# A steady step of a convolution and MLP kernel listed in another order, item by item

## Chip, core and metric

The kernel runs on one core of one Trainium2 chip. The metric is the time of one execution on the device in microseconds (us); lower is better. Each engine of the core works through its own list of instructions: TensorE (PE in the profile; PEld is its loading of weights), VectorE (DVE), ScalarE (ACT), GpSimd (POOL) and SyncE (SP, which only issues DMAs). They wait for one another through semaphores.

## What is computed

x is (8, 4096, 192), weight (8, 7), w_in (192, 2048), w_out (2048, 192), all float32.

```python
w = exp(weight - weight.max(-1));  w = w / (w.sum(-1) + 1e-9)      # 7 taps for each of 8 heads
x_pad = concatenate([zeros((B, 6, D)), x], axis=1)
out = einsum("hk,bskhg->bshg", w, x_unf)       # causal convolution, 24 channels to a head
x = out.reshape(32768, 192)
h = x @ w_in
g = h * (1.0 / (1.0 + exp(-1.702 * h)))
return g @ w_out                               # (32768, 192)
```

## The kernel before

The work goes in 32 steps ("big"), each of 512 tokens of two sequences, one sequence on either half of the partitions. Both matrix products are formed from fewer products of sums of blocks, so beside the products there are many sums and copies. The schedule is written out by hand: each engine gets its instructions in the order in which the program lists them.

One steady step has two parts. In the first, R below, the 20 products of `TERMS` are taken twice (two halves v of the hidden width) and each on two PSUM banks h = 0, 1: 80 matrix products of 64 x 128 by 64 x 512 (`product1`, line 598). The two banks of one product use the two row halves of the array. The results, named a0 to a8 while they lie in PSUM, are copied out by ScalarE (`copy2`, lines 633 and 635; k0 to k9 are rooms in SBUF), combined by VectorE (`sum2`, line 639) and put through the gelu by ScalarE (lines 615 and 620) into blocks of g. `ORDER` lists these items: `(0, "prod", 14, "a3")` is product 14 of half 0 into PSUM tile a3. An item there does both banks, h = 0 and then 1. Four PSUM tiles of two banks are handed out through the list `free`, in the order of first use.

In the second part, C below, the second product is taken: 78 "mains", each three matmuls of 128 x 32 by 256 on column strips 0 to 2 of the array, and 78 "sides", single matmuls on strip 3 (`one_matmul`, line 855). Mains and sides read g blocks and sums of them. These g sums, 128 x 1024 on VectorE (`add_up`, lines 355 and 357; `("sum", 6, 8, "-", 6)` in `PLAN`), stand partly in R (`EARLY_G`), and six more are accumulating DMAs ("acc", line 831) that GpSimd issues. `go(n)` takes n times one main and then one side, and where a side product ends, ScalarE's copy of it (line 880) stands right behind. "seed" is a copy by ScalarE between PSUM and rooms (line 884), "join" a sum of 96 x 256 on VectorE, "turn" a transpose of results by VectorE (line 771), "store" the DMA out.

Beside these, the convolutions of the next steps are made: x is transposed by VectorE (line 438), ScalarE multiplies it by each tap (line 483), GpSimd adds the taps of two channel groups (`next_add`, line 501) and issues accumulating DMAs for the third ("tree", line 506). Ten sums of the resulting blocks ("vsum", `next_sum`, lines 355 and 357, on GpSimd in steady steps) follow, and SyncE's DMAs "cross" copy blocks to the other half of the partitions. The queues `adds`, `tree`, `sums_left`, `pieces`, `todo` and `ready` hold these items in a fixed order, and "tap", "add", "vsum", "cross" and "done" in `ORDER` and `PLAN` take the next one of a queue.

The first steps (0 and 1) have a list of their own, `OPENING`, except that the second part of step 1 is made by `PLAN`.

## Time and profile before

| what | value |
|---|---|
| time, median of 3 runs | 2263.2 us (2262.88 to 2263.72) |
| time of the profiled execution | 2262.78 us |
| its span | 2261.1 us |
| DMA, mean over the span | 132 GB/s, 298.05 MB in all |
| ScalarE, GpSimd busy | 76%, 47% of the span |
| clock granted to TensorE | 1.0 |

A row of the profile gives the line of the kernel, the engine, the operation, "out<-in" by the program's names (a PSUM tile is a "slot"), and the shape; then a count. Groups give busy us and the mean ns of one. Rows of the timeline begin with start and length in us, and like instructions behind one another share a row. "<-" ahead of a name in brackets, or behind a wait, names what ended an engine's idle time.

### The profile page before, as it was taken

How to read it: one execution, taken by the hardware profiler on the slowest of the kernel's cores; microseconds unless marked ns; L12 is line 12 of the kernel's file. 1: busy time of each engine (PE TensorE's matmuls, PEld its weight loads, DVE VectorE, ACT ScalarE, POOL GpSimd, SP SyncE). 2: the span in 40 equal slices, each digit the busy share in tenths (PEclk: the TensorE clock that was granted, in tenths of full speed). 3: DMA queues.
4: the chain of work that ended last, by engine and by line, in shares of the span. 5: the costliest groups of instructions: out<-in, count | busy, mean ns of one | idle time of the engine just before them, and what ended most of it. 6: DMA issues, size and time to landing. Idle time of an engine off the chain costs nothing.

```text
span 2261.1 us, 62136 instructions
## 1 busy us (share of the span) xinstructions
PE 2248.2 (99%) x24966; PEld 1552.0 (69%) x24966; DVE 1985.3 (88%) x2970; ACT 1707.7 (76%) x3233; POOL 1063.9 (47%) x1098
## 2 busy tenths in 40 slices
...
GB/s 198 174 158 133 125 114 150 143 128 127 121 131 159 128 128 126 111 160 140 125 132 114 141 152 128 129 124 118 163 134 128 124 114 151 144 127 103 104 92 71
DMA packets 275679, 298.05 MB, mean 132 GB/s; under 512 B 119104, under 2 KB 203328, under 8 KB 275392
## 3 DMA queue, kind: packets, MB, share of 16 engines
...
q10 hardware_dynamic: 1648, 0.39, 0.1%
...
## 4 chain that ended last, share of the span: by engine, by line
PE 96%; DVE 2%; ACT 1%; issue 1%; DMA 1%; POOL 0%; DVEq 0%; ACTq 0%; POOLq 0%; SPq 0%
PE slot L598 49%; PE slot L855 45%; PE slot L1120 1%; DVE g L357 1%; DMA g<-osbs 0%; PE slot L1115 0%; DVE room L357 0%; ACT g L615 0%; PE slot L946 0%; DVE room L639 0%; ACT w_form L483 0%; DMA xin<-in_x_dram 0%; DVE slot L639 0%; DVE room L355 0%; DVE osbs L771 0%
## 5 line engine op out<-in xcount | busy, mean ns | idle before, releaser
L598 PE MATMUL slot<-conv_t,w_in_s 64*128 64x512 f32 x5152 | 1147.4, 594 | 3.3 <-ACT room L633 1.5
L598 PEld LDWEIGHTS slot<-conv_t,w_in_s 64*128 64x128 f32 x5152 | 663.3, 186 | 474.6 <-issue 312.1
L855 PE MATMUL slot<-g,w_form 128*32 128x256 f32 x9672 | 894.2, 379 | 0.7 <-DVE room L357 0.7
L855 PEld LDWEIGHTS slot<-g,w_form 128*32 128x32 f32 x9672 | 575.6, 110 | 128.9 <-DVE room L357 2.1
L501 POOL TENSOR_TENSOR conv_t<-conv_t,g 128x512 f32<-128x512 f32 x354 | 449.0, 1275 | 88.4 <-ACT g L483 65.4
L855 PE MATMUL slot<-g,w_out_s 128*32 128x256 f32 x5952 | 467.5, 379 | 1.3 <-DVE g L357 0.8
L357 DVE TENSOR_TENSOR g<-g 128x1024 f32<-128x1024 f32 x372 | 450.4, 1224 | 8.0 <-DMA g<-osbs 1.0
L880 ACT COPY room<-slot 32x256 f32<-32x256 f32 x651 | 237.2, 364 | 289.8 <-PE slot L855 281.5
L639 DVE TENSOR_TENSOR room<-slot,room 128x512 f32<-128x512 f32 x620 | 383.6, 679 | 67.8 <-PE slot L598 67.8
L633 ACT COPY room<-slot 128x512 f32<-128x512 f32 x620 | 337.7, 595 | 77.7 <-PE slot L598 61.7
L483 ACT ACTIVATE g<-xt,cw 128x512 f32<-128x512 f32 x534 | 353.9, 715 | 3.7
L620 ACT ACTIVATE g<-room 128x1024 f32<-128x1024 f32 x248 | 265.7, 1071 | 79.0 <-DVE room L639 49.3
L615 ACT ACTIVATE g<-slot 128x512 f32<-128x512 f32 x528 | 282.5, 610 | 51.9 <-PE slot L598 32.8
L831 POOL DMA_DIRECT2D g<-g x124 | 128.1, 1038 | 355.0 <-PE slot L855 330.8
L639 DVE TENSOR_TENSOR slot<-slot,room 128x512 f32<-128x512 f32 x372 | 239.7, 689 | 53.8 <-PE slot L598 52.2
L855 PEld LDWEIGHTS slot<-g,w_out_s 128*32 128x32 f32 x5952 | 239.7, 110 | 43.2 <-DVE room L639 23.3
L355 POOL TENSOR_TENSOR conv_t<-conv_t 128x256 f32<-128x256 f32 x210 | 179.3, 860 | 129.2 <-PE slot L598 119.6
L855 PE MATMUL slot<-osbs,w_form 128*32 128x256 f32 x2232 | 229.5, 379 | 0.0
L506 POOL DMA_DIRECT2D g<-g x120 | 105.9, 883 | 238.1 <-ACT g L483 99.4
L855 PEld LDWEIGHTS slot<-osbs,w_form 128*32 128x32 f32 x2232 | 132.5, 110 | 23.6
L639 DVE TENSOR_TENSOR slot<-room,slot 128x512 f32<-128x512 f32 x124 | 79.8, 687 | 41.8 <-PE slot L598 41.8
L855 PE MATMUL slot<-room,w_form 128*32 128x256 f32 x1488 | 112.9, 379 | 0.0
...
## 6 DMA issues: line engine op xcount, KB each, us to landing
...
conv_t<-conv_t SPq DMA_DIRECT2D x186, 192.0 KB, 5.4
...
conv_t<-conv_t SPq DMA_DIRECT2D x186, 128.0 KB, 2.9
out_dram<-osbs SPq DMA_DIRECT2D x186, 128.0 KB, 2.7
...
```

Of the source, the lines that this page charges most:

```text
L355: eng.tensor_add(v(dst), v(a), v(b))
L357: eng.tensor_sub(v(dst), v(a), v(b))
L483: act.mul(home, conv_src(big, c, k), cw[:, c, k : k + 1])
L501: nc.gpsimd.tensor_add(dst, dst, home)
L598: nc.tensor.matmul(slot[h], w_in_s[halves[h], a, v * P : (v + 1) * P], src, start=first, stop=True, skip_group_check=True,)
L615: act.activation(dst[:, :, h, :], src[h].rearrange("p (o t) -> p o t", o=2), AF.Gelu_apprx_sigmoid, scale=float(sign),)
L620: act.activation(dst.rearrange("p o h t -> p h o t"), src.rearrange("p h (o t) -> p h o t", o=2), AF.Gelu_apprx_sigmoid, scale=float(sign),)
L633: act.copy(bank(dst, h), bank(src, h))
L639: op(*(bank(t, h) for t in (dst, a, b)))
L831: nc.gpsimd.dma_start(out=spot(dst), in_=spot(a), accum_op=ALU.add)
L855: nc.tensor.matmul(dst, w, t, start=first, stop=last, skip_group_check=True)
L880: act.copy(to, d)
```

## The change

Steps 2 to 31 are no longer made by `ORDER`, `PLAN` and the queues, but by one list `STEP`, in which each item is one instruction (or the three matmuls of a main, or the two or more DMAs of a transfer). A flattened step of before and `STEP` hold the same 477 items. `OPENING` is written out in the same way, down to the end of step 1, in the order that it had.

In `STEP`, a product, copy, sum or gelu names its bank as its last entry (0 or 1; None for a gelu over both), and the banks of one product may stand apart. `("m", i)` is main i, `("s", i)` side i, `("t", i)` the copy of the i-th finished side; they no longer alternate. `("gsum", ...)` is a g sum. For items of the convolution the first number says how many steps ahead the item works: `("add", 1, 2, 5)` adds tap 5 of channel group 2 of the next step, `("vsum", 1, 9)` is its vsum 9. The three chunks of a side product lie in the strip-3 parts of three PSUM tiles; these are now taken in the order by, bx, bs in place of bx, bs, by.

The core of the diff:

```diff
-    ORDER = [
-        (0, "prod", 6, "a8"), (0, "sum", "k0", "a8", "-", "k8"), (0, "prod", 2, "a3"), (0, "copy", "k4", "a3", 1),
-        (0, "prod", 12, "a2"), ("tap",), ("tap",), ("tap",), ("tap",), ("add", 4), (0, "prod", 16, "a0"),
-        (0, "sum", "a1", "a2", "-", "k0"), ("add", 4), ("turn", 0), (0, "prod", 14, "a3"), (0, "copy", "k1", "a0", 1),
-        (0, "prod", 9, "a2"), (0, "sum", "a4", "a2", "-", "k1"), (0, "prod", 3, "a1"), (0, "copy", "k2", "a1", 1),
-        (0, "prod", 15, "a3"), (0, "prod", 7, "a4"), (0, "prod", 1, "a1"), (0, "sum", "k3", "a4", "+", "k4"),
-        ("add", 4), (0, "sum", "k5", "a1", "-", "k1"), (0, "prod", 18, "a2"), (0, "gelu", 1, 1, "a3", 1),
-        (0, "prod", 10, "a4"), ("turn", 1), (0, "gelu", 3, 1, "k3", 1), (0, "prod", 17, "a1"),
...
-        ("turn", 2), (1, "copy", "k4", "a3", 1), (0, "gelu", 3, 0, "k9", 1), (1, "prod", 12, "a2"), ("done",),
-        ("begin",), ("vsum",), (1, "prod", 16, "a0"), (1, "sum", "a1", "a2", "-", "k0"), (1, "prod", 14, "a3"),
-        (1, "copy", "k1", "a0", 1), ("g", 0), (1, "prod", 9, "a2"), (1, "sum", "a4", "a2", "-", "k1"),
-        (1, "prod", 3, "a1"), ("vsum",), ("vsum",), ("vsum",), ("vsum",), (1, "copy", "k2", "a1", 1),
-        (1, "prod", 15, "a3"), (1, "prod", 7, "a4"), ("vsum",), (1, "prod", 1, "a1"),
-        (1, "sum", "k3", "a4", "+", "k4"), (1, "sum", "k5", "a1", "-", "k1"), ("g", 1), (1, "prod", 18, "a2"),
...
-        (1, "gelu", 1, 1, "a3", 1), ("g", 2), (1, "prod", 10, "a4"), (1, "gelu", 3, 1, "k3", 1), ("g", 3),
-        (1, "prod", 17, "a1"), ("vsum",), (1, "copy", "a5", "a4", -1), (1, "copy", "k6", "a2", 1), ("vsum",),
-        (1, "prod", 19, "a4"), (1, "prod", 11, "a1"), ("vsum",), (1, "prod", 8, "a5"),
-        (1, "sum", "a6", "k6", "-", "a4"), (1, "prod", 5, "a4"), (1, "gelu", 0, 1, "a1", 1), ("g", 4),
-        (2, "prod", 0, "a3"), (1, "gelu", 1, 0, "a5", 1), (1, "sum", "a7", "a4", "+", "k2"),
-        (1, "gelu", 2, 1, "k5", 1), (1, "prod", 4, "a6"), (1, "prod", 13, "a4"), ("vsum",),
-        (1, "sum", "k7", "a7", "-", "k6"), (1, "sum", "k9", "a4", "-", "k0"), (1, "gelu", 0, 0, "a6", 1),
-        (1, "gelu", 2, 0, "k7", 1), ("cross",), (1, "gelu", 3, 0, "k9", 1), ("cross",), ("done",),
...
-    EARLY_G = [
-        (6, 6, "-", 10), (0, 5, "+", 6), (8, 0, "acc"), (1, 7, "-", 6), (1, 1, "-", 11),
...
-    PLAN = [
-        ("side", 13, 16, "k0"), ("main", 1, 5, "p2", 1), ("vsum",), ("go", 2), ("sum", 14, 14, "-", 18), ("go", 1),
-        ("vsum",), ("vsum",), ("go", 1), ("main", 16, 10, "p3", 0), ("go", 1), ("tap",), ("go", 1), ("vsum",),
-        ("go", 2), ("main", 0, 14, "p0", 1), ("go", 2), ("seed", "p4", "p2", 1), ("go", 1), ("seed", "k1", "p3", 1),
-        ("sum", 7, 8, "-", 7), ("sum", 8, 8, "-", 16), ("go", 1), ("sum", 5, 11, "-", 19), ("seed", "p5", "k1", 1),
...
-        mains, sides = (bs[0], bx[0], by[0]), (bx[1], bs[1], by[1])
...
-        def go(n):
-            for _ in range(n):
-                w, t = now["steps"].pop(0)
-                for c in range(NC):
-                    one_matmul(chunk(now["to"], c), w[:, chunk_cols(c)], t, now["first"], not now["steps"])
-                now["first"] = False
-                d, ws, ts, st, to = side.pop(0)
-                one_matmul(d, ws, ts, st, to is not False)
-                if to is not False:
-                    act.copy(to, d)
...
+    STEP = [
+        ("prod", 0, 6, "a8", 0), ("sum", 0, "k0", "a8", "-", "k8", 0), ("prod", 0, 12, "a2", 0),
+        ("prod", 0, 6, "a8", 1), ("sum", 0, "k0", "a8", "-", "k8", 1), ("prod", 0, 2, "a3", 1),
+        ("prod", 0, 2, "a3", 0), ("prod", 0, 12, "a2", 1), ("prod", 0, 16, "a0", 0), ("copy", 0, "k4", "a3", 1, 1),
+        ("tap", 1, 1, 6), ("copy", 0, "k1", "a0", 1, 0), ("prod", 0, 16, "a0", 1),
+        ("sum", 0, "a1", "a2", "-", "k0", 0), ("prod", 0, 9, "a2", 0), ("prod", 0, 14, "a3", 1),
+        ("sum", 0, "a1", "a2", "-", "k0", 1), ("prod", 0, 3, "a1", 0), ("prod", 0, 9, "a2", 1),
+        ("copy", 0, "k4", "a3", 1, 0), ("prod", 0, 15, "a3", 0), ("copy", 0, "k1", "a0", 1, 1),
...
+        ("prod", 0, 18, "a2", 1), ("prod", 0, 10, "a4", 0), ("copy", 0, "a5", "a4", -1, 0), ("prod", 0, 18, "a2", 0),
+        ("prod", 0, 10, "a4", 1), ("copy", 0, "a5", "a4", -1, 1), ("sum", 0, "k5", "a1", "-", "k1", 0),
...
+        ("gelu", 0, 0, 1, "a1", 1, 0), ("prod", 0, 8, "a5", 1), ("prod", 0, 8, "a5", 0),
...
+        ("add", 1, 1, 2), ("add", 1, 1, 3), ("add", 1, 1, 4), ("add", 1, 1, 5), ("osum", 1), ("vsum", 1, 0),
+        ("prod", 1, 12, "a2", 0), ("prod", 1, 12, "a2", 1), ("prod", 1, 16, "a0", 0), ("prod", 1, 16, "a0", 1),
+        ("add", 1, 2, 1), ("copy", 1, "k4", "a3", 1, 1), ("sum", 1, "a1", "a2", "-", "k0", 0),
+        ("prod", 1, 14, "a3", 1), ("cross", 1, 3, 4), ("prod", 1, 9, "a2", 0), ("gelu", 0, 2, 0, "k7", 1, None),
+        ("sum", 1, "a1", "a2", "-", "k0", 1), ("prod", 1, 9, "a2", 1), ("prod", 1, 3, "a1", 0), ("add", 1, 2, 2),
+        ("add", 1, 2, 3), ("copy", 1, "k1", "a0", 1, 0), ("copy", 1, "k4", "a3", 1, 0), ("copy", 1, "k1", "a0", 1, 1),
+        ("gsum", 6, 6, "-", 10), ("prod", 1, 3, "a1", 1), ("copy", 1, "k2", "a1", 1, 0),
+        ("gelu", 0, 3, 0, "k9", 1, None), ("copy", 1, "k2", "a1", 1, 1), ("prod", 1, 15, "a3", 1),
+        ("gelu", 1, 1, 1, "a3", 1, 1), ("sum", 1, "a4", "a2", "-", "k1", 0), ("add", 1, 2, 4),
...
+        ("copy", 1, "a5", "a4", -1, 0), ("prod", 1, 18, "a2", 0), ("prod", 1, 10, "a4", 1),
+        ("copy", 1, "a5", "a4", -1, 1), ("copy", 1, "k6", "a2", 1, 1), ("copy", 1, "k6", "a2", 1, 0),
+        ("prod", 1, 17, "a1", 1), ("prod", 1, 11, "a1", 1), ("gelu", 1, 0, 1, "a1", 1, 1), ("prod", 1, 17, "a1", 0),
+        ("prod", 1, 19, "a4", 0), ("prod", 1, 19, "a4", 1), ("prod", 1, 8, "a5", 0), ("prod", 1, 11, "a1", 0),
+        ("gelu", 1, 1, 0, "a5", 1, 0), ("gelu", 1, 0, 1, "a1", 1, 0), ("prod", 1, 8, "a5", 1),
+        ("gelu", 1, 1, 0, "a5", 1, 1), ("gsum", 1, 7, "-", 6), ("sum", 1, "a6", "k6", "-", "a4", 0),
+        ("prod", 1, 5, "a4", 0), ("sum", 1, "a6", "k6", "-", "a4", 1), ("prod", 1, 5, "a4", 1),
+        ("gsum", 1, 1, "-", 11), ("prod", 1, 4, "a6", 0), ("prod", 1, 4, "a6", 1), ("cross", 1, 4, 6),
+        ("prod", 2, 0, "a3", 1), ("sum", 1, "a7", "a4", "+", "k2", 0), ("prod", 2, 0, "a3", 0),
+        ("prod", 1, 13, "a4", 0), ("sum", 1, "a7", "a4", "+", "k2", 1), ("gelu", 1, 2, 1, "k5", 1, None),
+        ("sum", 1, "k7", "a7", "-", "k6", 0), ("prod", 1, 13, "a4", 1), ("sum", 1, "k7", "a7", "-", "k6", 1),
+        ("sum", 1, "k9", "a4", "-", "k0", 1), ("gelu", 1, 0, 0, "a6", 1, 1), ("sum", 1, "k9", "a4", "-", "k0", 0),
+        ("gelu", 1, 0, 0, "a6", 1, 0), ("begin", 0), ("gelu", 1, 2, 0, "k7", 1, None), ("s", 0), ("m", 0), ("s", 3),
+        ("s", 1), ("acc", 8, 0), ("gsum", 14, 14, "-", 18), ("s", 2), ("m", 4), ("gelu", 1, 3, 0, "k9", 1, None),
+        ("m", 5), ("vsum", 1, 1), ("s", 4), ("m", 2), ("s", 7), ("m", 1), ("vsum", 1, 2), ("gsum", 7, 8, "-", 7),
+        ("vsum", 1, 4), ("vsum", 1, 5), ("cross", 1, 6, 9), ("s", 8), ("tap", 2, 0, 0), ("vsum", 1, 3),
+        ("cross", 1, 9, 12), ("s", 9), ("s", 10), ("m", 3), ("m", 7), ("m", 6), ("s", 11), ("t", 0), ("s", 12),
+        ("s", 25), ("seed", "k1", "p3", 1), ("s", 5), ("m", 8), ("m", 9), ("s", 6), ("vsum", 1, 7), ("m", 10),
...
+        ("m", 37), ("t", 4), ("m", 32), ("join", "k7", "k1", "+", "k6"), ("s", 40), ("s", 52), ("s", 36), ("s", 51),
+        ("s", 53), ("tap", 2, 0, 4), ("acc", 18, 14), ("tap", 2, 0, 3), ("tree", 2, 0, 3, 4),
...
+        ("t", 7), ("load", 3), ("s", 37), ("s", 44), ("m", 45), ("gsum", 20, 20, "-", 11), ("tap", 2, 0, 2),
+        ("t", 10), ("m", 47), ("s", 45), ("t", 12), ("join", "k2", "k2", "-", "p2"), ("m", 53), ("t", 9), ("s", 41),
+        ("t", 11), ("m", 54), ("s", 48), ("gsum", 15, 15, "-", 16), ("m", 49), ("s", 46),
+        ("join", "k10", "p0", "-", "k9"), ("m", 57), ("m", 59), ("m", 50), ("m", 52), ("cross", 1, 0, 3),
+        ("tap", 2, 0, 5), ("gsum", 5, 7, "+", 15), ("s", 62), ("s", 63), ("s", 64), ("s", 47), ("s", 49), ("m", 48),
+        ("tap", 2, 0, 6), ("m", 51), ("tap", 2, 0, 1), ("m", 55), ("s", 54), ("s", 57), ("s", 67), ("vsum", 1, 9),
+        ("s", 56), ("seed", "p1", "k1", 1), ("gsum", 6, 14, "+", 6), ("gsum", 6, 6, "-", 17), ("t", 13),
...
+        ("tap", 2, 1, 4), ("tree", 2, 0, 5, 6), ("turn", 0, 0, 0, "k7"), ("vsum", 1, 8), ("s", 55), ("m", 69),
+        ("final",), ("m", 68), ("t", 15), ("s", 59), ("join", "k6", "k6", "+", "p4"), ("s", 60), ("t", 16),
+        ("join", "k2", "k2", "-", "k1"), ("end",), ("turn", 1, 1, 1, "k2"), ("m", 73), ("s", 69), ("s", 76),
+        ("tree", 2, 0, 0, 1), ("s", 74), ("m", 72), ("tap", 2, 1, 1), ("m", 70), ("m", 67), ("m", 66), ("s", 70),
+        ("tap", 2, 2, 1), ("turn", 1, 0, 0, "k6"), ("tap", 2, 1, 2), ("cross", 1, 12, 14),
+        ("join", "k1", "p3", "-", "k3"), ("m", 74), ("s", 66), ("s", 77), ("s", 75), ("t", 20),
+        ("turn", 0, 0, 1, "k1"), ("store", 0, 1), ("s", 73), ("m", 76), ("s", 71), ("join", "k2", "p2", "-", "k4"),
+        ("turn", 0, 1, 1, "k2"), ("m", 77), ("m", 75), ("join", "k1", "p5", "+", "k5"), ("t", 18), ("t", 19),
+        ("tap", 2, 2, 6), ("join", "k8", "k8", "+", "k0"), ("turn", 0, 1, 0, "k1"), ("turn", 1, 1, 0, "k8"),
+        ("store", 1, 0), ("cross", 1, 14, 16), ("tap", 2, 2, 4), ("tap", 2, 2, 5), ("tap", 2, 1, 5), ("store", 1, 1),
+        ("store", 0, 0), ("tree", 2, 0, 3, 5), ("tree", 2, 0, 0, 3),
...
+            t, dst, _ = args
+            product1(at(dst), *TERMS[t], big, v, (half, dst, h) not in begun, hs)
...
+    def begin(big):
+        bx, bs, by = (free.pop(0) for _ in range(3))
+        mains, sides = (bs[0], bx[0], by[0]), (by[1], bx[1], bs[1])
+        todo, aside, copies = [], [], []
+        now.update(big=big, tiles=(bx, bs, by), mains=mains, todo=todo, aside=aside, copies=copies, stored=[0, 0])
...
+    def main_part(i):
+        dst, w, t, first, last = now["todo"][i]
+        for c in range(NC):
+            one_matmul(chunk(dst, c), w[:, chunk_cols(c)], t, first, last)
+
+    def side_part(i):
+        d, w, t, first, to = now["aside"][i]
+        one_matmul(d, w, t, first, to is not False)
...
+    def end():
+        free.extend(now["tiles"][::2])
...
+    opening()
+    for big in range(2, N_BIG):
+        run(STEP, big)
```

702 lines of the change are left out of this document (267 added, 435 removed), and 250 rows, old and new, of tables (MAINS, OPENING, ORDER, PLAN).

## Prediction

> **What bounds the kernel now.** I read the page's engine totals and chain first, then a table of both stretches of one steady step beside one stretch of the opening, then the waits, then the timeline where two engines work side by side.
>
> ```profile
> span 2261.1 us, 62136 instructions
> ...
> PE 2248.2 (99%) x24966; PEld 1552.0 (69%) x24966; DVE 1985.3 (88%) x2970; ACT 1707.7 (76%) x3233; POOL 1063.9 (47%) x1098
> ...
> PE 96%; DVE 2%; ACT 1%; issue 1%; DMA 1%; POOL 0%; DVEq 0%; ACTq 0%; POOLq 0%; SPq 0%
> ```
>
> TensorE is busy 99% and the chain is 96% TensorE. The change removes no product, so it can only win what TensorE loses between products inside those 99%.
>
> ```profile
> core 0: us, PE busy (x) PEld busy (x) DVE busy (x) ACT busy (x) POOL busy (x), PEclk, DMA share, GB/s
> 136.80:172.97 36.17, 35.00 (x626) 23.04 (x626) 33.63 (x46) 24.99 (x52) 11.60 (x14) 1.00 0.79 154
> 1042.92:1076.87 33.95, 33.95 (x626) 28.69 (x625) 31.02 (x47) 24.82 (x52) 9.40 (x11) 1.00 0.79 154
> 1007.50:1042.92 35.42, 35.42 (x161) 20.68 (x160) 29.86 (x45) 28.71 (x50) 25.02 (x24) 1.00 0.54 112
> ```
>
> The third row is the first part of a steady step (R below: 80 first products, two passes each, on the two row halves of the array), the second row its second part (C: 78 mains of three column strips and 78 sides on the fourth, two passes each). One step is 35.42 + 33.95 = 69.37 us. The first row is the C of the last step of the opening, with the same 626 passes in 36.17 us. The clock is 1.00 in all.
>
> What a pass costs when nothing waits:
>
> ```profile
> L598 PE MATMUL slot<-conv_t,w_in_s 64*128 64x512 f32 x5152 | 1147.4, 594 | 3.3 <-ACT room L633 1.5
> ```
> ```profile
> 1012.66 1.88 PE L598 MATMUL slot<-conv_t,w_in_s 64*128 64x512 f32 x7
> ```
> ```profile
> 140.50 0.39 PE L855 MATMUL slot<-g,w_out_s 128*32 128x256 f32 x3
> 140.68 0.38 PE L855 MATMUL slot<-g,w_form 128*32 128x256 f32 x1
> 140.72 0.39 PE L855 MATMUL slot<-g,w_out_s 128*32 128x256 f32 x3
> 140.90 0.38 PE L855 MATMUL slot<-g,w_form 128*32 128x256 f32 x1
> 140.93 0.39 PE L855 MATMUL slot<-g,w_out_s 128*32 128x256 f32 x3
> ```
>
> R: seven passes on two halves are four behind one another on one of them, so a pass follows the last by (1.88 − 0.594) / 3 = 0.429 us. Each half takes 80 passes, 79 × 0.429 + 0.594 = 34.5 us at the least. R takes 35.42, so it loses **0.9 us** per step. C: passes of mains follow each other by 0.215 us (140.50, 140.72, 140.93), so 155 × 0.215 + 0.39 = 33.7 us at the least against 33.95. C has almost nothing to give and can only lose.
>
> The waits of weight loads inside this R (us in total, times, longest) say who is late:
>
> ```profile
> PEld slot L598 <- ACT room L633: 0.8, 3, 0.4
> ...
> PEld slot L598 <- ACT slot L635: 0.6, 3, 0.2
> PEld slot L598 <- DVE slot L639: 0.5, 2, 0.3
> PEld slot L598 <- POOL conv_t L501: 0.4, 1, 0.4
> ...
> PEld slot L598 <- DVE room L639: 0.2, 1, 0.2
> ```
>
> 2.5 us of waiting loads stand for 0.9 us of lost passes; the rest was covered by loads already done or by the other half. 1.4 of the 2.5 hang on ScalarE's copies out of PSUM.
>
> **What goes.** The steady step before and the new list hold the same 477 items, so no work is added or removed; only order moves. In R each product is now listed by bank half, and one half runs at most two ahead of the other. Product 14 waited for the copy "k4" of the bank that it overwrites; now products 16 and 9 stand between copy and product. Product 8 waited for the copy "a5", four half products ahead of it; now it is five to eight. So I let ScalarE's share of the waits go: 1.4 / 2.5 × 0.9 = **−0.5 us** per step (from −0.9, every wait gone, to 0, others in their place).
>
> **What comes.** VectorE is late next, and GpSimd makes it later. GpSimd's queue is what is moved most. The 12 tap adds all stood in the first half of R's list; now (2,1) to (2,4) stand in its second half, around the g sum (6,6,−,10). Of the ten sums of conv blocks ("vsums") nine were spread over R's second half and the tenth came at C's start; now seven are queued behind the accumulating DMA (8,0), which waits for the gelus of its g blocks, so they run as a burst at R's end, beside the g sums (1,7,−,6) and (1,1,−,11). Two more, 9 and 8, run in the middle and late part of C. What such a meeting costs:
>
> ```profile
> 140.86 2.36 DVE L357 TENSOR_TENSOR g<-g 128x1024 f32<-128x1024 f32 x2
> 143.14 2.32 DVE L357 TENSOR_TENSOR room<-g,osbs 128x1024 f32<-128x1024 f32 x1
> 145.38 1.21 DVE L355 TENSOR_TENSOR g<-g 128x1024 f32<-128x1024 f32 x1
> ```
> ```profile
> 143.34 1.03 POOL L355 TENSOR_TENSOR conv_t<-conv_t 128x256 f32<-128x256 f32 x1
> ```
> ```profile
> 153.98 0.42 PE L855 MATMUL slot<-g,w_out_s 128*32 128x256 f32 x3 [0.81 <-DVE g L357]
> ```
> ```profile
> 1104.62 1.40 DVE L355 TENSOR_TENSOR osbs<-g 128x1024 f32<-128x1024 f32 x1
> ...
> 1108.27 1.70 DVE L357 TENSOR_TENSOR osbs<-osbs,g 128x1024 f32<-128x1024 f32 x1
> ```
> ```profile
> 1102.71 2.22 POOL L355 TENSOR_TENSOR conv_t<-conv_t 128x256 f32<-128x256 f32 x3
> ...
> 1108.95 1.61 POOL L355 TENSOR_TENSOR conv_t<-conv_t 128x256 f32<-128x256 f32 x1
> ```
>
> A g sum alone takes 1.21 us; beside a vsum 1.40, 1.70 or 2.32 us. The vsum itself takes 1.03 or 1.61 us where three in a row take 2.22 / 3 = 0.74. After that meeting in the opening's C, TensorE stands still for 0.81 us waiting for a g sum, and that C is 36.17 − 33.95 = 2.2 us longer than a steady one. So one meeting costs VectorE between +0.2 (1.40 − 1.21) and +1.1 us (2.32 − 1.21), of which none to all comes through to TensorE. A tap add beside a g sum is not among these rows; the same two ends bound it.
>
> ```profile
> L501 POOL TENSOR_TENSOR conv_t<-conv_t,g 128x512 f32<-128x512 f32 x354 | 449.0, 1275 | 88.4 <-ACT g L483 65.4
> L639 DVE TENSOR_TENSOR room<-slot,room 128x512 f32<-128x512 f32 x620 | 383.6, 679 | 67.8 <-PE slot L598 67.8
> ```
>
> The Trainium skill, "SBUF — State Buffer", section "SBUF: two separate sides", says that VectorE's second port pair is shared with GpSimd under an exclusive lock: a VectorE operation with two SBUF inputs and a GpSimd operation wait for each other to the end. The rows of 1108 agree, where both grow. By that rule a g sum that meets an add waits up to the add's 1.275 us, and its term below would be +1.3 in place of +0.2, the sum 2305.
>
> Per step, with R's VectorE busy 29.86 of 35.42 us and C's 31.02 of 33.95:
> - The g sum (6,6,−,10) beside adds in R: 0 to +1.1. The 5.6 us that VectorE is free in R cover most; taken at **+0.2**, the smaller meeting.
> - R's end. Product 13 of the second half overwrites the bank that sum "a7" reads. Between product 5, which fills that bank, and product 13 lie two products of each half, 2 × 2 × 0.429 = 1.7 us; in that time product 5 has to come out (0.594) and two sums of 0.679 to follow, 1.95 together. So 0.25 us is short there, and all that the burst adds to the g sum just ahead comes on top. Of the two g sums there one is at 1.70 today; with the other at 1.70 too, +0.5. From 0 to +1.1; taken at **+0.3**, nearest to the 0.25.
> - Vsum 9 stands on GpSimd behind the tree sum (3,4), which waits for the tap (0,3) in C's middle, so it meets the g sums (20,20) or (15,15) listed there, which mains read: 0 to +1.1, taken at **+0.2**, since VectorE has 2.9 us free in C. Vsum 8 lies among short joins: nothing.
> - Mains and sides come in runs of up to six, and side copies stand some items behind their sides, so joins may get them later: 0 to +0.3, taken at **+0.1**.
>
> ```profile
> conv_t<-conv_t SPq DMA_DIRECT2D x186, 192.0 KB, 5.4
> ```
>
> At nothing: the side strips' banks in another order (the same copies from other banks, and ScalarE is free 9 of 33.95 us in C); the later crosses (at most 5.4 us each, issued before R, and block 14 is first read 26 half products into R, 13 × 0.86 = 11 us); x transposes and the load, which are read in the next step; the stores now together at the step's end, whose buffer is written again in R's second half; the other accumulating DMAs, which keep their distance to readers. Without its cover each would cost its own wait, and only the accumulating DMAs, queued on GpSimd ahead of vsums, stand near one.
>
> Sum: −0.5 + 0.2 + 0.3 + 0.2 + 0.1 = **+0.3 us** per step. The opening's order is the same in both kernels. With 30 steady steps, +9 us on the profiled execution's 2262.78 us (span 2261.1 and 1.7 around it), which is 0.4 below the median of 2263.2. **Forecast 2272 us.**
>
> **The rivals.** *The waits go and the meetings stay covered.* For it: VectorE's 5.6 free us in R. Against: the waits on VectorE that PE has there already. −0.5 × 30: **2248 us**; with the whole 0.9 gone, 2236.
>
> *A wash:* gains and meetings cancel to within 0.15 us a step, **2259 to 2267**.
>
> *TensorE's queue is too short for the runs* (slower by another mechanism). Counted along C's list, sides run up to five matmuls ahead of mains, mains up to three ahead of sides. If only four of one kind could queue while the other strips still work, six matmuls of C's longer runs would exceed that, each for up to its two passes, 0.43 us: up to 2.6 us per C, half of it taken (1.3 × 30), **2302 us**. It decides where fewer than five are held. The rows from 140.50 show strips interleaved in single passes, so they don't settle it.
>
> *Strict order.* 78 of the 155 neighbours in C's list take the same strip, and 22 of the 79 in R the same half. If passes started only in listed order, each would cost a pass: 78 × 0.215 + 22 × 0.429 = 26 us a step, **3050 us**. Against it: in the rows from 140.50 a side's pass starts between any two main passes, so also between the two passes of one main, where the listed order has none. The Trainium skill, "TensorE: Matmul & The Clock Gate", section "The mechanism", states this rule, matmuls "strict FIFO, no reordering"; these rows do not agree with it, at least by one pass.
>
> *No effect,* every queue coming out as before, is excluded: the order differs on every engine.
>
> **How the numbers follow.** 0.2% (4.5 us, 0.15 us a step) is about what a measurement here can tell from no change. Slower: 0.45, of which the forecast 0.39, the short queue 0.05, strict order 0.01. Waits gone: 0.38. A wash: 0.17. Range: its low end is −0.5 a step, 2247; its high end little gained and one meeting in full (−0.1 + 1.1), +1.0 a step, 2292. Forecast case alone: 2268 to 2292. Outside lie strict order, most of the short queue, and some 0.14 beyond the ends.
>
> **What would show it.** Right: R between 35.0 and 35.6 with no wait on ScalarE's copies of product 14; one or more of the g sums (6,6,−,10), (1,7,−,6), (1,1,−,11) at 1.6 us or more; C above 34.1 with VectorE as releaser; PE waits on VectorE where they were on ScalarE. Wrong: R near 34.6 and C at 33.95 (waits gone), or strips idle in C that nothing releases (queue).

## The result, and the profile after

| | median | lowest to highest | runs |
|---|---|---|---|
| before | 2263.04 us | 2262.21 to 2263.72 | 4 |
| after | 2416.1 us | 2415.45 to 2417.69 | 4 |

The ratio is 1.0678, with a 95% interval of 1.0659 to 1.0696: 153 us slower, 5.1 us in each of the 30 steady steps. From here on, the length of R and C is the median over a kernel's steady steps, from the first start of a product to the first start of a main or side and on to the next product, taken from all starts in the trace. By this measure R went from 35.42 to 35.17 us and C from 33.94 to 39.41 us. All of the loss, and more, is in C.

In the new kernel's profile helper lines have moved: products of R are L483, mains and sides L744, ScalarE's side copies L780, its other PSUM copies L537, taps L446, gelus L500, sums L343 and L345, accumulating DMAs L533, the load of x L78. First the page: span, engine totals and the chain.

```profile
span 2416.0 us, 61546 instructions
...
PE 2379.8 (99%) x24966; PEld 1513.3 (63%) x24966; DVE 2030.8 (84%) x2970; ACT 1719.8 (71%) x3233; POOL 1102.0 (46%) x1098
...
PE 76%; DMA 10%; DVE 7%; ACT 4%; issue 2%; SPq 0%; DVEq 0%; ACTq 0%
```

TensorE is still "busy" 99% with the same 24966 passes, though it is busy for 132 us more: this number counts time in which any strip of the array works, and cannot show that strips stand idle. The chain is 10% DMA, where it was 1%.

The table of stretches, for one steady step (C first, then the R before it):

```profile
core 0: us, PE busy (x) PEld busy (x) DVE busy (x) ACT busy (x) POOL busy (x), PEclk, DMA share, GB/s
1029.30:1068.23 38.93, 38.35 (x626) 24.09 (x624) 33.41 (x46) 24.50 (x51) 12.32 (x16) 1.00 0.91 187
994.12:1029.30 35.18, 35.18 (x165) 23.54 (x161) 29.43 (x46) 29.43 (x50) 24.18 (x22) 1.00 0.26 52
```

C moves 187 GB/s where it moved 154, R 52 where it moved 112: the load of x now runs in C. TensorE stands wholly still for only 0.58 us of this C, which is 5 us longer than before's. The rest has to be sought strip by strip, in TensorE's timeline of that C:

```profile
1031.51 0.39 PE L744 MATMUL slot<-g,w_out_s 128*32 128x256 f32 x3
1031.69 0.38 PE L744 MATMUL slot<-g,w_form 128*32 128x256 f32 x1
1031.72 0.39 PE L744 MATMUL slot<-g,w_out_s 128*32 128x256 f32 x3
1031.91 0.81 PE L744 MATMUL slot<-g,w_form 128*32 128x256 f32 x3
1032.35 0.42 PE L744 MATMUL slot<-g,w_out_s 128*32 128x256 f32 x3
```

"x3" of `w_out_s` is one pass of a main on its three strips, `w_form` a pass of a side. Main passes follow each other by 0.21 us, then there is none from 1031.72 to 1032.35, while three side passes run alone. No releaser is named there, but the profile names one only where the whole engine stands idle, so that alone proves nothing; the order of the starts does. The list there reads `("s", 8) ... ("s", 9), ("s", 10), ("m", 3)`. Of the three lone passes, two end side 8 and the third, at 1032.34, is the first of side 9; main 3 starts with it. At that moment sides 9 and 10 still have four passes to start. I counted over all starts of this C: wherever a main or a side starts over 0.1 us late without a semaphore (8 mains, 6 sides), it starts when exactly four passes listed ahead of it on another strip are still to start, the one that starts at that moment among them. Mains lose 3.9 us and sides 3.5 us in this way.

The other new thing is in the waits inside this C:

```profile
ACT g L446 <- DMA g<-g: 2.6, 1, 2.6
...
PEld slot L744 <- ACT room L780: 1.1, 1, 1.1
...
PE slot L744 <- ACT room L780: 0.6, 1, 0.6
```

Once per C, a tap on ScalarE stands 2.6 us for an accumulating DMA that still reads the g block which the tap overwrites. The side copies are queued behind it on ScalarE, and TensorE waits for the PSUM bank that they empty. In the list of DMAs the accumulating ones take 9.5 us to land where before they took 6.5:

```profile
g<-g POOLq DMA_DIRECT2D x124, 512.0 KB, 9.5
```

And SyncE's timeline shows what they meet. It runs ahead of the place in the list, so the load starts 2.2 us after C does:

```profile
1031.50 4.23 SPq L78 DMA_DIRECT2D xin<-in_x_dram  x8
```

So two suspects: the runs of mains and sides, and the place of the load. Last, the g sums that were to meet GpSimd's sums, in VectorE's timeline, and the vsum beside the last of them in GpSimd's:

```profile
1015.81 1.22 DVE L345 TENSOR_TENSOR g<-g 128x1024 f32<-128x1024 f32 x1
...
1022.70 1.22 DVE L345 TENSOR_TENSOR osbs<-g 128x1024 f32<-128x1024 f32 x1
...
1025.52 1.34 DVE L345 TENSOR_TENSOR osbs<-osbs,g 128x1024 f32<-128x1024 f32 x1
...
1053.80 3.15 DVE L343 TENSOR_TENSOR g<-g 128x1024 f32<-128x1024 f32 x2
```
```profile
1053.68 1.04 POOL L343 TENSOR_TENSOR conv_t<-conv_t 128x256 f32<-128x256 f32 x1
```

In R they take 1.22 to 1.34 us, hardly above the 1.21 us alone; only the pair in C pays, 3.15 us for two in place of 2.42. That does not mean that nothing met in R. The first of them, at 1015.81, lies inside a row of four adds on GpSimd:

```profile
1014.53 6.33 POOL L450 TENSOR_TENSOR conv_t<-conv_t,g 128x512 f32<-128x512 f32 x4
```

Eight adds earlier in the same R take 10.62 us, so four would take 5.3: here GpSimd lost the 1.0 us of the meeting, and VectorE nothing. The burst of seven vsums at R's end came too. It began at 1023.94, when the g sum of 1022.70 had just ended, and the one of 1025.52 met a vsum, which took 1.59 us in place of 0.73.

### The profile page after: what moved, and what is told of

Same layout as the page of the kernel before. It is cut to its first block, busy times and chain, and to the rows that moved or that the text cites. A ratio compares the mean times of both kernels' runs of the same rounds, so it can differ in the third digit from the quotient of the medians.

```text
span 2416.0 us, 61546 instructions
## 1 busy us (share of the span) xinstructions
PE 2379.8 (99%) x24966; PEld 1513.3 (63%) x24966; DVE 2030.8 (84%) x2970; ACT 1719.8 (71%) x3233; POOL 1102.0 (46%) x1098
## 4 chain that ended last, share of the span: by engine, by line
PE 76%; DMA 10%; DVE 7%; ACT 4%; issue 2%; SPq 0%; DVEq 0%; ACTq 0%
PE slot L483 46%; PE slot L744 30%; DMA g<-g 10%; DVE g L345 3%; DVE room L345 2%; ACT g L446 2%; ACT room L780 1%; DVE g L343 1%; ACT g L500 0%; DMA xin<-in_x_dram 0%; ACT w_form L446 0%; ACT conv_t L1119 0%; DVE xt L407 0%; DVE room L343 0%; ACT w_form L539 0%
## 5 line engine op out<-in xcount | busy, mean ns | idle before, releaser
L483 PE MATMUL slot<-conv_t,w_in_s 64*128 64x512 f32 x5152 | 1139.5, 595 | 3.2 <-ACT room L537 1.5
L744 PE MATMUL slot<-g,w_form 128*32 128x256 f32 x9672 | 1028.4, 381 | 21.6 <-ACT room L780 17.1
L483 PEld LDWEIGHTS slot<-conv_t,w_in_s 64*128 64x128 f32 x5152 | 746.9, 186 | 383.0 <-issue 149.9
L744 PEld LDWEIGHTS slot<-g,w_form 128*32 128x32 f32 x9672 | 520.5, 110 | 347.1 <-ACT room L780 33.8
L537 ACT COPY room<-slot 128x512 f32<-128x512 f32 x806 | 404.9, 541 | 297.0 <-PE slot L744 197.4
L744 PE MATMUL slot<-g,w_out_s 128*32 128x256 f32 (+1 forms) x6048 | 537.0, 385 | 1.9 <-DVE g L345 0.8
L450 POOL TENSOR_TENSOR conv_t<-conv_t,g 128x512 f32<-128x512 f32 x354 | 479.8, 1359 | 60.9 <-ACT g L446 40.0
L345 DVE TENSOR_TENSOR g<-g 128x1024 f32<-128x1024 f32 x372 | 449.2, 1228 | 17.9 <-PE slot L744 15.7
L446 ACT ACTIVATE g<-xt,cw 128x512 f32<-128x512 f32 x534 | 354.5, 717 | 88.0 <-DMA g<-g 84.0
L345 DVE TENSOR_TENSOR room<-slot,room 128x512 f32<-128x512 f32 x620 | 365.0, 626 | 12.1 <-PE slot L744 0.9
L780 ACT COPY room<-slot 32x256 f32<-32x256 f32 x651 | 229.9, 366 | 175.4 <-PE slot L744 163.9
L500 ACT ACTIVATE g<-slot 128x512 f32<-128x512 f32 x528 | 295.6, 601 | 35.0 <-PE slot L483 31.3
L744 PE MATMUL slot<-osbs,w_form 128*32 128x256 f32 x2232 | 318.0, 381 | 0.0
L500 ACT ACTIVATE g<-room 128x1024 f32<-128x1024 f32 x248 | 263.5, 1062 | 59.4 <-DVE room L345 24.6
L533 POOL DMA_DIRECT2D g<-g x124 | 107.6, 867 | 414.8 <-PE slot L744 205.2
L744 PEld LDWEIGHTS slot<-g,w_out_s 128*32 128x32 f32 x6048 | 224.9, 109 | 66.9 <-DVE room L345 2.0
L343 DVE TENSOR_TENSOR room<-slot,room 128x512 f32<-128x512 f32 (+1 forms) x248 | 133.6, 549 | 109.9 <-PE slot L744 75.2
L343 POOL TENSOR_TENSOR conv_t<-conv_t 128x256 f32<-128x256 f32 x210 | 222.0, 1065 | 7.4 <-DVE conv_t L441 0.4
L345 DVE TENSOR_TENSOR slot<-slot,room 128x512 f32<-128x512 f32 x248 | 163.5, 693 | 37.2 <-ACT room L537 29.9
L744 PEld LDWEIGHTS slot<-osbs,w_form 128*32 128x32 f32 x2232 | 135.1, 110 | 59.0
L345 POOL TENSOR_TENSOR conv_t<-conv_t 128x256 f32<-128x256 f32 x120 | 88.6, 750 | 173.9 <-PE slot L483 169.2
```

The costliest lines, as they stand in the source:

```text
L343: eng.tensor_add(v(dst), v(a), v(b))
L345: eng.tensor_sub(v(dst), v(a), v(b))
L446: act.mul(tap_home(big, c, k), conv_src(big, c, k), cw[:, c, k : k + 1])
L450: nc.gpsimd.tensor_add(tap_home(big, c, 0), tap_home(big, c, 0), tap_home(big, c, k))
L483: nc.tensor.matmul(slot[h], w_in_s[halves[h], a, v * P : (v + 1) * P], src, start=first, stop=True, skip_group_check=True,)
L500: act.activation(dst, src, AF.Gelu_apprx_sigmoid, scale=float(sign))
```

## The experiments

They are told by question; the number in a label is the order in which they ran. Ratios are to before. R and C are measured as above. Diffs are shown in part: "..." marks lines left out, and a line may stop before its end.

| run | what | median us | ratio (95%) | R | C |
|---|---|---|---|---|---|
| e1 | before, strip-3 banks as after | 2263.83 | 1.0005 (0.9996 to 1.0014) | 35.62 | 33.81 |
| e2 | before's order, after's runs of m and s | 2392.48 | 1.0573 (1.0557 to 1.0589) | 35.6 | 38.13 |
| e3 | after, m and s in turn | 2354.5 | 1.042 (1.0397 to 1.0444) | 35.21 | 37.33 |
| e4 | before with after's products, copies, sums, gelus of R | 2355.89 | 1.0412 (1.0397 to 1.0428) | 38.86 | 33.81 |
| e5 | e3 with the load in R | 2264.74 | 1.0009 (1.0 to 1.0018) | 35.21 | 34.11 |
| e6 | e3 with three taps later | 2334.94 | 1.0318 (1.0303 to 1.0333) | 35.27 | 36.51 |
| e7 | after's R, before's C | 2331.39 | 1.0304 (1.0283 to 1.0324) | 36.5 | 35.7 |
| e8 | before's order, six sides then six mains | 2650.46 | 1.1713 (1.169 to 1.1737) | 35.6 | 46.77 |
| e9 | after with the load in R | 2400.9 | 1.0612 (1.0597 to 1.0626) | 35.17 | 38.87 |
| e10 | e7 with the load in R | 2274.03 | 1.005 (1.0038 to 1.0063) | 35.19 | 34.51 |
| e11 | before with the load in C | 2261.39 | 0.9995 (0.9986 to 1.0004) | 35.42 | 33.94 |
| e12 | before's order, four sides then four mains | 2328.58 | 1.0291 (1.0272 to 1.031) | 35.6 | 35.99 |
| e13 | e9 with no lead over two | 2274.69 | 1.0053 (1.0037 to 1.007) | 35.17 | 34.52 |
| e14 | e3 with the load at C's end | 2273.57 | 1.005 (1.0035 to 1.0065) | 35.5 | 34.11 |
| e15 | e10 with two vsums and a cross moved | 2251.43 | 0.9949 (0.9935 to 0.9962) | 35.05 | 33.94 |

### The parts of the change

e1 writes before's order as one list and changes only the banks of strip 3; e2 keeps that list, with before's banks, and puts only the mains and sides into after's pattern of runs, each kind in its own order (and the copies "t" with their sides).

```diff
-        mains, sides = (bs[0], bx[0], by[0]), (bx[1], bs[1], by[1])
+        mains, sides = (bs[0], bx[0], by[0]), (by[1], bx[1], bs[1])
```
```diff
-        ("m", 0), ("s", 0), ("m", 1), ("s", 1), ("gsum", 14, 14, "-", 18), ("m", 2), ("s", 2), ("m", 3),
+        ("s", 0), ("m", 0), ("s", 1), ("s", 2), ("gsum", 14, 14, "-", 18), ("s", 3), ("m", 1), ("m", 2),
...
```

> The order of the kernel before, written as one list, with only the side strips' banks taken as by, bx, bs. Both theories (full strip queues; late copies and DMAs) put this at no difference: 2263 us within 4. If the banks matter, side copies wait for another bank's main and C (33.95 us before) grows.

> The order of the kernel before, old banks, but mains and sides follow the new list's pattern of runs (s m s s s m m ...) in place of strict alternation; nothing else moves. Theory 'full strip queues' (only four passes listed for one strip can wait; a further one blocks all that is listed behind it): the other strips idle as in the changed kernel, C near 37.5 to 38.5 us, 2365 to 2400 us. Theory 'late copies and DMAs' (the accumulating DMAs at 9.5 us, taps waiting for them on ScalarE, side copies behind): C stays at 33.9 to 34.2, 2263 to 2270 us.

The banks cost nothing that can be measured. The runs alone cost 128.7 us over e1 (2392.48 − 2263.83), 4.3 us in each C (38.13 − 33.81), with nothing else of the change present; over before itself it is 130 us. In the table of stretches a C of e2 has TensorE busy without a gap:

```profile
1020.80:1058.93 38.13, 38.13 (x626) 24.23 (x626) 31.36 (x45) 24.76 (x52) 10.22 (x12) 1.00 0.71 138
```

So these 4.3 us are not more passes (626): they lie less densely. By the median over 29 C's of e2, the matmuls that start when exactly four passes listed ahead of them on another strip are still to start account for all of it: 4.33 us on the mains' strips and as much on the sides', and nothing else there is late by more than 0.03 us.

e3 is the converse: after, but one main and one side in turn (the copies "t" moved along with their sides).

```diff
-        ("s", 0), ("m", 0), ("s", 3), ("s", 1), ("acc", 8, 0), ("gsum", 14, 14, "-", 18), ("s", 2), ("m", 4),
+        ("m", 0), ("s", 0), ("m", 4), ("s", 3), ("acc", 8, 0), ("gsum", 14, 14, "-", 18), ("m", 5), ("s", 1),
...
```

> The changed kernel with mains and sides listed strictly in turn again (each in the new list's own sequence); all other engines keep the new order. 'Full strip queues': C falls from 39.4 to 34 to 35 us, in all 2255 to 2285 us. 'Late copies and DMAs': C stays above 38 us, 2390 us or more.

Taking the runs out gives back only 61.6 of the 153 us, so neither forecast held. With them gone, C is still 3.4 us too long, and now the waits of the whole run show it:

```profile
ACT g L446 <- DMA g<-g: 117.3, 28, 5.0
...
PEld slot L744 <- ACT room L780: 77.3, 82, 1.4
...
PE slot L744 <- ACT room L780: 40.3, 54, 0.9
```

That is the tap behind the accumulating DMA, 28 times, and TensorE behind ScalarE. ScalarE's timeline of one C has both: the tap waits 3.98 us, and the side copies come behind it.

```profile
1030.26 1.34 ACT L446 ACTIVATE g<-xt,cw 128x512 f32<-128x512 f32 x2 [3.98 <-DMA g<-g]
1031.62 0.76 ACT L780 COPY room<-slot 32x256 f32<-32x256 f32 x2
```

e4 puts only R's products, PSUM copies, PSUM sums and gelus into after's order, and leaves VectorE's g sums and x transposes, GpSimd's work and C where before has them.

```diff
-        ("prod", 0, 6, "a8", 0), ("prod", 0, 6, "a8", 1), ("sum", 0, "k0", "a8", "-", "k8", 0),
+        ("prod", 0, 6, "a8", 0), ("sum", 0, "k0", "a8", "-", "k8", 0), ("prod", 0, 12, "a2", 0),
...
```

> The order of the kernel before with only the products, copies, PSUM sums and gelus of the first part in the new order, bank by bank; convolution items and the whole second part as before. If the new order of the products is what took R from 35.48 to 35.17 us, R is 35.1 to 35.25 here and the time 30 x 0.3 = 9 us below: 2250 to 2257 us. If the gain came from moving GpSimd's and the g sums' items, R stays at 35.4 or more: 2261 us or more.

A clear miss: R became 3.3 us longer, not shorter. Its waits over the run:

```profile
PEld slot L483 <- DVE slot L345: 83.6, 152, 1.9
PEld slot L483 <- DVE room L345: 53.7, 90, 1.2
```

In after the first of these is much smaller:

```profile
PEld slot L483 <- DVE slot L345: 33.0, 88, 1.9
```

As a part by itself the new order of R's products is a loss. By these waits it needs the new places of the g sums and transposes on VectorE, but no run moves those alone.

### The runs: how much a strip holds

e8 and e12 make the runs regular, in e1's list with before's banks: groups of six sides and then six mains, or of four and four. The fences leave out the items of other engines between them, which keep their order.

```diff
-        ("m", 0), ("s", 0), ("m", 1), ("s", 1), ("m", 2), ("s", 2), ("m", 3), ("s", 3), ("m", 4), ("s", 4), ("m", 5), ("s", 5),
+        ("s", 0), ("s", 1), ("s", 2), ("s", 3), ("s", 4), ("s", 5), ("m", 0), ("m", 1), ("m", 2), ("m", 3), ("m", 4), ("m", 5),
...
```
```diff
-        ("m", 0), ("s", 0), ("m", 1), ("s", 1), ("m", 2), ("s", 2), ("m", 3), ("s", 3),
+        ("s", 0), ("s", 1), ("s", 2), ("s", 3), ("m", 0), ("m", 1), ("m", 2), ("m", 3),
...
```

> The kernel before with sides and mains listed in groups of six sides, then six mains. Theory 'four passes for each strip': mains of a group start when four passes of its sides are left, sides of the next group when four passes of mains are left, so a group takes 4 x 6 - 8 = 16 passes in place of 12: 13 groups x 16 x 0.216 = 45 us per C in place of 33.9, about 2590 us. Rival 'sixteen passes shared by all strips': a group's mains and sides run beside each other, C 34 to 35.5 us, 2265 to 2310 us. Rival 'strict order': sides and mains take turns of twelve passes, 13 x 24 x 0.216 = 67 us, about 3250 us.

> The kernel before with sides and mains listed in groups of four and four. If four passes of one strip can wait, a group takes 4 x 4 - 8 = 8 passes, as many as in turn, and only the last mains end some four passes later: C 34.5 to 35.2, 2280 to 2305 us. If only two can wait, a group takes 4 x 4 - 4 = 12 passes in place of 8: C near 50, 2750 us. If none can, strict order, 16 passes: C 67.

TensorE's timeline at the start of a C, six and six, then four and four:

```profile
1115.03 2.10 PE L744 MATMUL slot<-g,w_form 128*32 128x256 f32 x9
1116.76 0.42 PE L744 MATMUL slot<-g,w_out_s 128*32 128x256 f32 x3
```
```profile
997.20 1.24 PE L744 MATMUL slot<-g,w_form 128*32 128x256 f32 x5
998.07 0.42 PE L744 MATMUL slot<-g,w_out_s 128*32 128x256 f32 x3
```

Six sides are twelve passes. The first main starts 1.73 us after them, which is eight passes of 0.216: with the ninth, so that four are still to start. Four sides are eight passes; the first main starts after 0.87 us, with the fifth, and again four are still to start. Whatever the length of the group, it is four passes, that is two float32 matmuls of two passes each, that can be passed by. (Every matmul here has two passes, so the runs can't tell whether passes or matmuls are counted.) In groups of six one turn (six sides, six mains) takes 3.53 us where twelve passes one behind another take 2.6: each kind stands still for four passes of every turn (16 x 0.2156 = 3.45), and some 0.075 us is left over. In the groups of four a turn takes 1.80 us where eight passes take 1.73. The starts show where the remainder lies: a matmul that was held starts 0.03 us (a side) or 0.05 us (a main) after the moment that the rule gives, and its second pass follows the first by 0.26 or 0.24 us in place of 0.216. With it both C's add up from e1's 33.81 us: 12 held mains of 0.937 us and the first main's 1.73 us make 46.8 for e8, and 18 of 0.073 and the first main's 0.87 make 36.0 for e12; measured were 46.77 and 35.99. Why a held matmul loses these 0.07 us stays open.

e9 moves only the load in after, back into R behind the third x transpose of its first half, and leaves the runs.

```diff
-        ("xt", 2, 2), ("prod", 1, 0, "a3", 1),
+        ("xt", 2, 2), ("load", 3), ("prod", 1, 0, "a3", 1),
...
-        ("t", 7), ("load", 3), ("s", 37),
+        ("t", 7), ("s", 37),
```

> The changed kernel, runs of mains and sides kept, with only the load of x moved back to the first part. With both causes there it took 2416 us, with the runs taken out 2354, with both taken out 2265. Theory 'two causes': what is left are the runs, worth some 126 us in the order of before (C 38.13 against 33.94): C 38 to 38.6, 2380 to 2400 us, so that the load costs less beside runs than without them (some 25 us against 90), since TensorE idles for the runs while the DMAs land. If the two simply add, 2326 us; if the load is the only real cause, 2265.

With the runs in place, the load is worth only 15.2 us (2416.1 − 2400.9), and the runs, against e5 below, 136.2 us. e13 then keeps e9's runs as they are, but moves a main or a side forward wherever one kind would be listed more than two matmuls ahead of the other; 52 of the 155 neighbours in C's list still take the same strip.

```diff
-        ("s", 9), ("s", 10), ("m", 3), ("m", 7), ("m", 6), ("s", 11), ("t", 0), ("s", 12), ("s", 25),
+        ("m", 3), ("s", 9), ("m", 7), ("s", 10), ("m", 6), ("s", 11), ("t", 0), ("m", 8), ("s", 12),
...
```

> The changed kernel with the load in the first part (2401 us with the new list's runs, 2265 in strict turn), and the mains and sides in the new list's pattern of runs except that neither kind is ever listed more than two matmuls ahead of the other: 52 of 155 neighbours still take the same strip. Theory 'four passes for each strip': a lead of two matmuls is four passes and costs nothing, C 34.0 to 34.4, 2262 to 2270 us. Rival 'each same-strip neighbour costs': 52 of the 78 remain, two thirds of the 136 us, about 2355 us.

126.2 us come back (2400.9 − 2274.69), and C goes from 38.87 to 34.52 us. So it is the lead of one kind, not that neighbours take the same strip. The 10 us that are left over e5 are more than expected. In e13 a median of 11 matmuls in each C still start when exactly four passes listed ahead of them are to start, and lose 0.45 us (sides) to 0.58 us (mains), mostly the 0.07 us above; e5, in strict turn, has none of these starts. That is the size of the difference, as e13's C is 0.41 us longer than e5's. A lead of two matmuls is thus at the limit and not yet free.

### The load

e5 is e3 with the load back in R, the same edit as in e9; e6 leaves the load in C and moves the taps (0,4), (0,3), (0,2) and a tree sum behind up to six more side copies; e14 moves the load to C's end, behind the last cross.

```diff
-        ("tap", 2, 0, 4), ("acc", 18, 14), ("tap", 2, 0, 3), ("tree", 2, 0, 3, 4),
+        ("acc", 18, 14),
...
-        ("gsum", 20, 20, "-", 11), ("tap", 2, 0, 2), ("t", 10),
+        ("gsum", 20, 20, "-", 11), ("t", 10),
...
-        ("t", 11), ("gsum", 15, 15, "-", 16),
+        ("t", 11), ("tap", 2, 0, 4), ("tap", 2, 0, 3), ("tree", 2, 0, 3, 4), ("tap", 2, 0, 2), ("gsum", 15, 15, "-", 16),
```
```diff
-        ("t", 7), ("load", 3), ("m", 45),
+        ("t", 7), ("m", 45),
...
-        ("store", 1, 0), ("cross", 1, 14, 16), ("tap", 2, 2, 4),
+        ("store", 1, 0), ("cross", 1, 14, 16), ("load", 3), ("tap", 2, 2, 4),
```

> The run with mains and sides in turn again (2354 us), and the load of x moved from the second part back into the first, behind the x transposes. Theory 'crowded DMAs': the load's 1.4 MB beside the accumulating DMAs of the second part is what takes these from 5.8 to 10.0 us, and the tap on ScalarE that waits for one of them holds the side copies behind it; without the load they take 6 to 7 us, ScalarE's wait of 4 us for a DMA shrinks below 1 us, C falls from 37.3 to 34 to 35.5 us, 2255 to 2300 us in all. Rival 'order on ScalarE alone': the accumulating DMAs stay late because their own issue is late; C stays at 36.5 us or more, 2330 us or more.

> The run with mains and sides in turn again (2354 us), with the load where the new list has it, and the three taps (0,4), (0,3), (0,2) of the next step but one listed behind the six side copies that stood behind them. Both theories agree that ScalarE then copies the sides without waiting for a DMA: C falls from 37.3 to 34 to 35.5 us, 2255 to 2300 us. If C stays above 36.5 us, it is something other than these copies that is late (a join, a g sum).

> Mains and sides in turn (2354 us with the load early in the second part, 2265 with it in the first), the load at the end of the second part, behind the last cross. Theory 'crowded DMAs': it no longer meets the six accumulating DMAs, which take 6 to 7 us again, C 34.0 to 34.6, 2260 to 2275 us. If the load hurts anywhere in the second part (by the crosses behind it on SyncE, or the x transposes that wait for it), 2300 us or more.

e5 is 89.8 us faster than e3 by that one item, and level with before. Stretches of C in e3, with the load, and in e5, without it (the last two columns are the share of the DMA engines and GB/s):

```profile
1013.00:1017.00 4.00, 4.00 (x80) 2.45 (x76) 4.00 (x4) 2.21 (x6) 0.87 (x1) 1.00 1.15 232
...
1021.00:1025.00 4.00, 4.00 (x80) 2.45 (x76) 3.59 (x4) 2.34 (x8) 0.86 (x1) 1.00 1.13 243
...
1029.00:1033.00 4.00, 2.60 (x39) 1.05 (x30) 3.97 (x6) 2.67 (x5) 1.11 (x3) 1.00 1.07 216
```
```profile
976.00:980.00 4.00, 4.00 (x80) 2.37 (x76) 4.00 (x5) 2.22 (x7) 0.87 (x1) 1.00 0.82 187
```

With the load, the share of the DMA engines reads 1.05 to 1.15 from 4 to 24 us into C; in e5 the same five stretches read 0.71 to 1.04. The accumulating DMAs land later, and 20 to 24 us into C only 39 passes start in 4 us in place of 80: there TensorE waits for the PSUM banks behind the late tap. What an accumulating DMA takes to land, from the lists of DMAs of e3, e5 and e11:

```profile
g<-g POOLq DMA_DIRECT2D x124, 512.0 KB, 10.0
```
```profile
g<-g POOLq DMA_DIRECT2D x124, 512.0 KB, 6.2
```
```profile
g<-g POOLq DMA_DIRECT2D x124, 512.0 KB, 8.0
```

The taps' wait of 117.3 us in e3 is gone with the load, in e5:

```profile
ACT g L446 <- DMA g<-g: 2.5, 4, 1.2
```

e14 confirms it from the other end: with the load behind C's DMAs they take 6.2 us, the taps wait 2.0 us in all and C is 34.11, as in e5. Its time is 8.8 us above e5's because R takes 35.5 us in place of 35.21. e6 was a miss. Moving the taps away saved 20 of the 90 us, since it gave new waits: the seeds of PSUM are now queued behind the taps, and TensorE waits for those (3.8 us for the first of these rows in e3).

```profile
PEld slot L744 <- ACT slot L537: 53.9, 41, 1.8
...
PE slot L744 <- ACT slot L537: 36.6, 28, 1.3
```

What else is in e6's C, which varies from 36.0 to 39.9 us while there are loads, I have not settled.

e11 asks whether the load alone does it: before, with the load in C's list, so that SyncE issues it 2.1 us ahead of C's start (1040.69):

```profile
1038.61 4.07 SPq L78 DMA_DIRECT2D xin<-in_x_dram  x8
```

```diff
-        ("load", 3), ("copy", 1, "k4", "a3", 1, 0),
+        ("copy", 1, "k4", "a3", 1, 0),
...
-        ("m", 45), ("s", 45), ("t", 12),
+        ("m", 45), ("s", 45), ("load", 3), ("t", 12),
```

> The kernel before with only the load of x moved into the second part, at the same count of mains and sides as in the new list. Theory 'crowded DMAs': accumulating DMAs at 8 to 10 us in place of 5.8, taps and mains late, C 35 to 37.5: 2290 to 2370 us. If the load only hurts together with the new list's order on ScalarE, C stays below 34.3: 2263 to 2272 us.

It does not: the accumulating DMAs take 8.0 us there, the taps wait 0.2 us for them in the whole run, and the time is that of before. But the new places of the taps are not needed for the harm: e7 below has C's taps and accumulating DMAs where before has them, all but the accumulating DMA (8,0), and there the load costs 57 us and the taps wait again:

```profile
ACT g L446 <- DMA g<-g: 89.0, 27, 3.8
```

In e7 the load starts 2.2 us after C does, some 4 us later than in e11, it meets the accumulating DMA (8,0) and two crosses that stand at C's start, and R is after's; the accumulating DMAs take 9.1 us. Which of these makes the difference to e11 no run tells.

### What the new first part is worth

e7 joins after's R to before's C; what after has moved from R into C (the accumulating DMA (8,0), nine vsums, two crosses, the load) stands in one block at C's start. e10 is e7 with the load in R. e15 is e10 with vsums 9 and 8 taken out of that block and put where after has them, late in C. The cross (14,16), which stood in C's middle in e10, goes to C's end with them, so e15 moves three items and not two.

```diff
+        ("acc", 8, 0), ("vsum", 1, 1), ("vsum", 1, 2), ("vsum", 1, 4), ("vsum", 1, 5), ("cross", 1, 6, 9),
+        ("vsum", 1, 3), ("cross", 1, 9, 12), ("vsum", 1, 7), ("vsum", 1, 6), ("load", 3), ("vsum", 1, 8),
+        ("vsum", 1, 9), ("m", 0), ("s", 0), ("m", 1), ("s", 1),
...
```
```diff
-        ("vsum", 1, 8), ("vsum", 1, 9), ("m", 0), ("s", 0),
+        ("m", 0), ("s", 0),
...
-        ("cross", 1, 0, 3), ("m", 59), ("s", 59),
+        ("vsum", 1, 9), ("cross", 1, 0, 3), ("m", 59), ("s", 59),
...
-        ("m", 66), ("s", 66),
+        ("m", 66), ("vsum", 1, 8), ("s", 66),
...
-        ("cross", 1, 14, 16), ("m", 47), ("s", 47),
+        ("m", 47), ("s", 47),
...
+        ("s", 77), ("cross", 1, 14, 16), ("t", 20), ("turn", 0, 1, 1, "k2"), ("store", 1, 1),
...
```

> The whole first part of the new list (every engine's items of it) and the second part of the kernel before; what the new list had moved from the first part to the second (accumulating DMA 8,0, vsums 1 to 9, two crosses, the load) stands at the second part's start. If the first part's gain is its own, R is 35.2 and C 33.9 to 34.2: 2253 to 2262 us, faster than both kernels. If the crowd of DMAs at the second part's start or the vsums beside its g sums cost more, C is 34.5 or more and the time 2270 us or more.

> The new list's first part and the second part of before, as in the run of 2331 us, with the load in the first part again. Theory 'crowded DMAs': R 35.2, C 33.9 to 34.3, 2253 to 2262 us, below both kernels. Rival: the crosses and vsums that come late into the second part keep it slow: C 34.8 or more, 2275 us or more.

> The run of 2274 us (the new list's first part with the load in it, the second part of before), with vsums 9 and 8 and the cross that carries them taken from the second part's start to the places late in it that the new list gives them. Theory 'vsums beside g sums': the first four g sums of the second part take 4.8 us again in place of 6.08, C falls from 34.51 to 33.95 to 34.1, R stays at 35.19: 2255 to 2260 us, below both kernels. Rival: C's excess has another cause (crosses, the accumulating DMA 8,0): C stays at 34.4 or more, 2270 us or more.

Between e7 and e10 lie 57 us for the load once more, about half of them in R (36.5 us against 35.19). But e10, expected near before, came out 11 us slower. What it loses shows beside GpSimd's vsums: VectorE's first four g sums of C, in before, in e10 with GpSimd's row, and in e15.

```profile
1044.18 4.76 DVE L357 TENSOR_TENSOR g<-g 128x1024 f32<-128x1024 f32 x4
```
```profile
977.99 6.08 DVE L345 TENSOR_TENSOR g<-g 128x1024 f32<-128x1024 f32 x4
```
```profile
978.46 3.39 POOL L343 TENSOR_TENSOR conv_t<-conv_t 128x256 f32<-128x256 f32 x2
```
```profile
968.99 5.15 DVE L345 TENSOR_TENSOR g<-g 128x1024 f32<-128x1024 f32 x4
```

The four take 6.08 us beside two vsums and 5.15 us where those are gone (4.8 was expected, as two earlier vsums still run beside the first). TensorE's weight loads wait less for VectorE's sums, in e10 and in e15 over the whole run:

```profile
PEld slot L745 <- DVE room L345: 57.0, 90, 1.3
```
```profile
PEld slot L744 <- DVE room L345: 26.4, 37, 1.3
```

What the cross adds to that was not tried by itself, nor is it known why R, expected to stay at 35.19 us, fell to 35.05. e15 is 22.6 us faster than e10 and beats both kernels of this change: 2251.43 us, 0.9949 of before with an interval of 0.9935 to 0.9962. Its step in the table of stretches, R and then C:

```profile
932.60:967.65 35.05, 35.05 (x161) 21.98 (x160) 29.97 (x45) 28.96 (x50) 24.07 (x22) 1.00 0.48 99
967.65:1001.65 34.00, 34.00 (x626) 24.71 (x624) 32.04 (x46) 24.74 (x52) 11.89 (x15) 1.00 0.83 165
```

By the medians R is 0.37 us shorter than before's and C as long: 0.37 x 30 = 11 us, against 11.4 measured (2262.81 − 2251.43).

## Why the prediction was wrong

**The sign was right, the size was not,** and the sign was luck: the meetings on which "slower" rested did not slow TensorE in R, which became shorter. What happened was the rival that had 0.05, and beside it a cost that the sum had at nothing.

**The short queue.** The mechanism was named rightly, and also how it would look: "strips idle in C that nothing releases". Its size failed twice. "If only four of one kind could queue" counted matmuls; it is four passes, two matmuls. So in the C shown not six matmuls were held by up to 0.43 us, but 14 by 0.4 to 1.3 us. And the price, "half of it taken (1.3 × 30)", came out at 4.3 us a C in e2 and 4.8 in e9 against e5, so 129 to 136 us and not 39. The step that failed before that is the range. Before's C has no lead of more than one matmul of either kind, so nothing in its trace could show the depth of this queue. An unknown that is bounded only by "no cost" on one side and 3050 us on the other belongs in the range, and the forecast should not have rested on it at 0.05.

**The load.** The step "At nothing: … x transposes and the load, which are read in the next step; … the other accumulating DMAs, which keep their distance to readers" failed. It asked when the load is read, not what it meets. Its cover was argued for the reader of x; the cost is with the accumulating DMAs (6.2 to 10.0 us) and the taps that overwrite what these read. By e3 against e5 it is 89.8 us, second only to the runs; beside the runs it shows as 15.2 us only. A C that is 4.8 us longer may give the DMAs that time; this was not tried. The list's place also misled: it stands in C's middle, but SyncE got there 2.2 us after C's start.

**R.** The sum for it was −0.5 + 0.2 + 0.3 = 0; measured −0.25 us. "R between 35.0 and 35.6" held. But the reason given is not confirmed. The waits of weight loads inside the R of 994.12 are these:

```profile
PEld slot L483 <- ACT room L537: 1.1, 3, 0.4
PEld slot L483 <- DVE slot L345: 1.0, 3, 0.6
...
PEld slot L483 <- DVE room L345: 0.4, 2, 0.2
PEld slot L483 <- ACT g L500: 0.2, 1, 0.2
```

Together 2.7 us, no less than before's 2.5, with 1.3 on ScalarE. What made R shorter was not isolated. And the meetings cost VectorE at most 0.13 us: the g sums named take 1.22 to 1.34 us, not 1.6 or more, since one met nothing and beside the adds it was GpSimd that lost the 1.0 us. Two terms, too large by about the same, cancelled; that R came out inside its bounds is luck. e4 adds that R's order is no sum of parts.

**Vsum 9 in C** did meet a pair of g sums (+0.73 us on VectorE), but a later one than said: the two at 1053.80 are sums with a plus (L343), (5,7,+,15) and (6,14,+,6), while (20,20) and (15,15) before them took 1.21 and 1.22 us. And vsum 8, put at "nothing", made a join of 96 x 256 beside it take 1.31 us in place of 0.42. Whether any of the 0.2 us reached TensorE can't be read in a C that is 5 us longer; e10 against e15 suggests that such meetings, in a C that is otherwise tight, do.

**Banks and side copies.** The banks at nothing: confirmed by e1. "C above 34.1 with VectorE as releaser": above, but with ScalarE behind a DMA as releaser, and mostly none.

**Strict order** is refuted: 78 neighbours on one strip in C cost 4 to 5 us, not 78 × 0.215 = 16.8, and in R, with 22, nothing. e13 has 52 such neighbours and loses 0.4 us a C against e5. The order is strict only beyond four passes.
